# Three head pairs at the start of an attention kernel: loads on two hardware queues, rotation on VectorE, and a new order of the preparation

## The chip, the cores and the metric

The kernel runs on one core of a Trainium2 chip. The metric is the device time of one execution in microseconds (us); a time is the median of several runs. A trace of one execution tells what each engine did: PE (TensorE, matrix products and transposes; PEld is its weight loads), DVE (VectorE), ACT (ScalarE), POOL (GpSimd) and SP (SyncE, which only issues DMAs). ACT and POOL can issue DMAs too; "SPq" and "ACTq" are such issues. A difference of about 0.5% (2.6 us) is what a measurement of this kernel can tell from no change.

## The reference

Attention over 2 batches of 8 heads (sequence 576, head dimension 64) with a rotation of q and k, then a gated feed-forward block, then a second one with softmax gating and a normalisation:

```python
def rotate(x):
    x1, x2 = (x[..., :half], x[..., half:])
    return np.concatenate([x1 * cos - x2 * sin, x1 * sin + x2 * cos], axis=-1)
q_rot, k_rot = (rotate(q), rotate(k))
scores = scale * np.matmul(q_rot, k_rot.transpose(0, 1, 3, 2))
scores = scores - np.max(scores, axis=-1, keepdims=True)
attn = np.exp(scores)
attn = attn / (np.sum(attn, axis=-1, keepdims=True) + 1e-09)
return np.matmul(attn, v).astype(np.float32)
...
x = _moe_ref(x=x, **moe_kwargs)          # (x @ w_a) * (x @ w_b) @ w_out
return _moe2_ref(x=x, **moe2_kwargs)     # gated by softmax, normalised, times w_out
```

All is in float32; a product is made of three passes over values split into a high part, which TensorE takes as it is, and a low part, the rest.

## The kernel before

The 16 heads are worked on as eight pairs, numbered 0 to 7. A pair has nine blocks of 128 query rows: 0 to 3 of the first head, 5 to 8 of the second, and block 4 with the last 64 rows of both. So q and k of a pair lie in SBUF as nine blocks too, and are loaded in three parts: A (blocks 0 to 3), B (5 to 8) and R (block 4). The R part is a DMA of its own with 64 rows of each head.

Ahead of a pair's scores stands its preparation. q and k are rotated by `rope`: a product of the swapped halves with the sines into `t2`, a product with the cosines in place, and a sum. `k_hi` (ACT) and `k_lo` write the two parts of k side by side into `kd`. q is needed twice side by side in `qd`: for pairs 1 to 7 `q_twice` copies it with a DMA from SBUF to SBUF on SP's queue, for pair 0 the rotation's sum is made twice. PE then transposes `kd` and `qd` (tiles `qtkA`, `qtkB`, `qtqA`, `qtqB`, `qtR`), and ACT and DVE write the results, split, into `kS` and `qS`. In pairs 1 to 7 the rotation, `k_lo` and the low part of v run on POOL.

Then, block by block (n = 9 u + i for block i of pair u): scores `s` on PE, the row's maximum `nm` on DVE, the exponential `e` on ACT, its transposes `t` on PE, the high part of them on ACT and the low part on DVE (both into `pT`), and at four places of a pair nine products `pv` with v. At a pair's end the sums of the rows are turned into reciprocals (`sums` on DVE, `rs` on PE, `rr` on ACT), which three DMAs spread over the partitions by way of DRAM (`rd`, then `rb`, all on SP's queue); POOL multiplies the pair's output `x` with them. After the eight pairs come the feed-forward blocks, which the change leaves alone.

All of attention is put in order by hand: every step is added with a position, a number in units of one block, and all steps are sorted by it. `PLAN` holds the positions of a pair, 9 u being added; `FIRST`, `SECOND` and `THIRD` replace some for pairs 0, 1 and 2. Each engine, and each DMA queue, runs its instructions strictly in that order. The tiles `kraw`, `qd` and `kd` have two buffers each.

Before, `start` issues the loads of pair 0's k and the tables of cosines and sines (one tile `cs`), with q of pair 0 on POOL's queue, and right behind them on SP's queue the loads of pair 1 and the rest of pair 0. POOL rotates pair 1 as soon as that is there, while DVE rotates pair 0: part A and R at first, part B (`rope_k5`, `rope_q5`) between the first blocks' work.

Of the kernel before, what the change touches and what calls it, by code (L numbers as in the profile page):

```python
# [107 lines left out]
def attention_gated_ffn_solu_ffn(ctx: ExitStack, tc, q, k, v, wa, wb, wo1, wi2, wo2, gln, rope_cs, out):  # L108

    nc = tc.nc  # L110
    const = ctx.enter_context(tc.tile_pool(name="const", bufs=1))
# [65 lines left out]
    nm, e, sums, ps, tt, x0, rb = {}, {}, {}, {}, {}, {}, {}  # L177

    def load(u, nm_, parts="ABR", eng=nc.sync):

        b, h0 = u // NP, 2 * (u % NP)
        if nm_ == "k":
            src = k
            if u not in kraw:
                kraw[u] = at.tile([P, NB, D], F32, tag="kraw", name=f"kraw{u}")
            t = kraw[u]
        else:
            src = q  # L190
# [23 lines left out]
    def rope(eng, u, x, nm_, lo=0, hi=NB):  # L214
        t2 = at.tile([P, NB, D], F32, tag="t2" if u else "t2first", name=f"t2{nm_}{lo}_{u}", bufs=2 if u else 1)
        x, t2, c, s = (ap[:, lo:hi] for ap in (x, t2, c_sb, s_sb))
        swapped = x.rearrange("p b (j d) -> p b j d", j=2)[:, :, ::-1, :]
        t2, s = (ap.rearrange("p b (j d) -> p b j d", j=2) for ap in (t2, s))
        eng.tensor_tensor(t2, swapped, s, op=ALU.mult)
        t2 = t2.rearrange("p b j d -> p b (j d)")  # L220
        eng.tensor_tensor(x, x, c, op=ALU.mult)
        if nm_ == "q" and u == 0:
            eng.tensor_tensor(qd[u][:, lo:hi, 0, :], x, t2, op=ALU.add)
        eng.tensor_tensor(x, x, t2, op=ALU.add)

    def q_twice(u):
        nc.sync.dma_start(out=qd[u][:, :, 0, :], in_=qd[u][:, :, 1, :])
# [264 lines left out]
    def add(pos, fn, *args):  # L492
        ops.append((pos, len(ops), fn, args))

    def start():
# [18 lines left out]
        nc.scalar.copy(cs[:, :, 5:9], cs[:, :, 0:4])  # L514

        t = ps_t.tile([P, 4, P], F32, tag="t", name="warm")
        for i in range(28):
            nc.tensor.transpose(t[:, i % 4], ident, ident)
# [7 lines left out]
    engines = {"dve": nc.vector, "pool": nc.gpsimd}  # L526
    for part, (lo, hi) in (("0", (0, 5)), ("5", (5, 9))):
        pos = {key: FIRST[key + part] for key in ("rope_k", "k_hi", "k_lo", "rope_q")}
        add(pos["rope_k"], lambda lo, hi: rope(nc.vector, 0, kraw[0], "k", lo, hi), lo, hi)
        add(pos["k_hi"], k_hi, 0, lo, hi)  # L530
        add(pos["k_lo"], k_lo, 0, engines[HI["l" + part]], lo, hi)
        eng = engines[HI["q" + part]]
        add(pos["rope_q"], lambda lo, hi, eng: rope(eng, 0, qd[0][:, :, 1, :], "q", lo, hi), lo, hi, eng)
# [353 lines left out]
```

## Time and profile before

| | |
|---|---|
| Time, median of 3 runs | 524.66 us (524.63 to 526.62) |
| The profiled execution's own time | 524.1 us |
| Its span, first to last instruction | 522.0 us |
| Granted TensorE clock, mean | 0.986 |
| Attention | from the start to about 179 us |
| First row maximum (block 0) | starts at 16.90 us |
| First row maximum of pair 1, 2, 3 | 35.87, 56.69, 76.09 us |
| DVE busy from 40 to 60 us | 19.2 of 20 us |

A row of the timeline has start, duration, engine, line, operation, output and inputs with their shapes, the count, and in brackets how long the engine had been idle and what ended that. A row of stretches has, for each engine, its busy time and in brackets the number of its instructions, then the granted clock, the busy share of the DMA engines and what they moved.

### The profile page before, as it was taken

How to read it: one execution, taken by the hardware profiler on the slowest of the kernel's cores; microseconds unless marked ns; L12 is line 12 of the kernel's file. 1: busy time of each engine (PE TensorE's matmuls, PEld its weight loads, DVE VectorE, ACT ScalarE, POOL GpSimd, SP SyncE). 2: the span in 40 equal slices, each digit the busy share in tenths (PEclk: the TensorE clock that was granted, in tenths of full speed). 3: DMA queues.
4: the chain of work that ended last, by engine and by line, in shares of the span. 5: the costliest groups of instructions: out<-in, count | busy, mean ns of one | idle time of the engine just before them, and what ended most of it. 6: DMA issues, size and time to landing. Idle time of an engine off the chain costs nothing.

```text
span 522.0 us, 7983 instructions
## 1 busy us (share of the span) xinstructions
PE 490.2 (94%) x2992; PEld 461.7 (88%) x2992; DVE 389.7 (75%) x603; ACT 270.1 (52%) x554; POOL 178.6 (34%) x128
## 2 busy tenths in 40 slices
PE   3889989989989999999999999999999969999997
PEld 3878888989878999999999999999999858888886
DVE  5899999999999776666756656655899996755450
ACT  2698988989988535433434443321455533222221
POOL 5598987877244003211111221220054221000000
PEclk9699999999999999999999999999999989999999
DMA  6334224235003053322222221343545200100011
GB/s 147 79 94 104 67 60 109 62 74 158 24 2 105 1 161 124 119 82 82 80 83 94 76 91 62 94 148 95 180 130 162 82 0 1 40 21 21 21 40 40
DMA packets 50914, 41.97 MB, mean 80 GB/s; under 512 B 23765, under 2 KB 46868, under 8 KB 50876
## 3 DMA queue, kind: packets, MB, share of 16 engines
q1 hardware_dynamic: 50124, 40.48, 26.1%
q10 hardware_dynamic: 624, 0.82, 0.5%
q8 instruction: 23, 0.38, 0.3%
q0 software_dynamic: 128, 0.17, 0.2%
q14 instruction: 15, 0.12, 0.1%
HBM read 37.00 MB, written 2.39 MB: 75 GB/s over the span
## 4 chain that ended last, share of the span: by engine, by line
PE 70%; DVE 19%; ACT 4%; issue 3%; DMA 2%; POOL 1%; SPq 1%; ACTq 0%; POOLq 0%; DVEq 0%
PE ab L579 29%; PE x L710 10%; PE out L814 10%; PE h L743 7%; PE pv L403 5%; PE s L327 4%; DVE nm L336 3%; PE t L354 2%; DVE f L93 2%; DVE f L95 2%; ACT e L344 2%; DVE pT L372 2%; DVE f L91 1%; PE lt L785 1%; DVE V L233 1%
## 5 line engine op out<-in xcount | busy, mean ns | idle before, releaser
L579 PE MATMUL ab<-xT,wab 128*128 128x384 f32 x864 | 151.9, 336 | 0.0
L579 PEld LDWEIGHTS ab<-xT,wab 128*128 128x128 f32 x864 | 150.7, 188 | 0.1
L710 PE MATMUL x<-gT,wx 128*128 128x384 f32 x432 | 75.9, 336 | 0.0
L710 PEld LDWEIGHTS x<-gT,wx 128*128 128x128 f32 x432 | 75.6, 188 | 0.1
L104 POOL TENSOR_TENSOR wab<-f,wab 128x1024 fp32r<-128x1024 f32 x11 | 26.4, 2401 | 118.9 <-ACT wab L101 103.0
L327 PE MATMUL s<-kS,qS 128*128 128x288 f32 x320 | 60.0, 315 | 1.3 <-ACT e L344 1.2
L743 PE MATMUL h<-wh,xT 128*128 128x512 f32 x216 | 53.2, 403 | 5.0 <-DVE et L763 5.0
L344 ACT ACTIVATE e<-s,nm 128x576 f32<-128x576 f32 x72 | 53.6, 745 | 7.1 <-DVE nm L336 6.5
L336 DVE TENSOR_REDUCE nm<-s 128x1 f32<-128x576 f32 x72 | 53.7, 745 | 2.1 <-PE s L327 1.2
L743 PEld LDWEIGHTS h<-wh,xT 128*128 128x128 f32 x216 | 41.5, 193 | 15.1 <-issue 4.9
L814 PE MATMUL out<-wout,lnT 128*128 128x512 f32 (+1 forms) x240 | 52.9, 373 | 0.0
L372 DVE TENSOR_TENSOR pT<-t,pT 128x512 fp32r<-128x512 f32 x72 | 49.4, 686 | 2.4 <-ACT pT L368 1.4
L327 PEld LDWEIGHTS s<-kS,qS 128*128 128x128 f32 x320 | 47.2, 195 | 3.7 <-ACT e L344 3.0
L814 PEld LDWEIGHTS out<-wout,lnT 128*128 128x128 f32 x240 | 41.4, 188 | 7.5
L403 PE MATMUL pv<-pT,V 128*128 128x288 f32 x288 | 46.0, 304 | 0.8 <-DVE pT L390 0.7
L354 PE MATMUL t<-ident,e 128*128 128x128 f32 x288 | 44.2, 277 | 0.0
L368 ACT CAST pT<-t 128x512 fp32r<-128x512 f32 x72 | 42.2, 586 | 2.5 <-PE t L354 2.1
L403 PEld LDWEIGHTS pv<-pT,V 128*128 128x128 f32 x288 | 39.4, 188 | 2.0 <-POOL V L251 0.7
L587 ACT COPY a<-ab 128x384 f32<-128x384 f32 x36 | 17.3, 480 | 45.3 <-PE ab L579 44.6
L596 DVE TENSOR_TENSOR gT<-a,gT 128x384 fp32r<-128x384 f32 x36 | 23.1, 641 | 21.8 <-ACT gT L595 21.8
L89 DVE TENSOR_SCALAR f<-f 128x512 f32<-128x512 f32 (+2 forms) x36 | 28.7, 796 | 12.3 <-ACT f L87 12.2
L756 ACT ACTIVATE et<-h,mx 128x1024 f32<-128x1024 f32 x9 | 10.1, 1117 | 52.2 <-DVE mx L755 52.2
(132 smaller groups left out, 714.4 us busy)
## 6 DMA issues: line engine op xcount, KB each, us to landing
raw<-in_moe_w_a_dram SPq DMA_DIRECT2D x12, 512.0 KB
raw<-in_moe_w_b_dram SPq DMA_DIRECT2D x12, 512.0 KB
raw<-in_moe_w_out_dram SPq DMA_DIRECT2D x8, 768.0 KB
raw<-in_moe_w_in_dram SPq DMA_DIRECT2D x8, 512.0 KB
raw<-in_moe_w_out_dram SPq DMA_DIRECT2D x8, 512.0 KB
kraw<-in_k_dram SPq DMA_DIRECT2D x16, 128.0 KB
vraw<-in_v_dram SPq DMA_DIRECT2D x8, 256.0 KB
qd<-qd SPq DMA_DIRECT2D x7, 288.0 KB
```

What stands on the lines that cost most here:

```text
L89: eng.tensor_scalar(_raw(t), _raw(t), LOW_END, HIGH_END, op0=ALU.max, op1=ALU.min)
L327: nc.tensor.matmul(s[:, c, :KC], qS[u % 2][:, a, off:off + P], kS[u % 2][:, h, c * KC:(c + 1) * KC], start=(m == 0), stop=(m == last),)
L336: nc.vector.tensor_reduce(t, ps[n][:, :, :KC], axis=AX.XY, op=ALU.max, negate=True)
L344: nc.scalar.activation(t.rearrange("p (c n) -> p c n", c=2), ps.pop(n)[:, :, :KC], AF.Exp, bias=nm.pop(n), accum_out=sums[u][:, i:i + 1],)
L354: nc.tensor.transpose(t[:, j, :], e[n][:, j * P:(j + 1) * P], ident)
L368: nc.scalar.copy(hi, src)
L372: nc.vector.tensor_tensor(lo, src, _raw(hi), op=ALU.subtract)
L403: nc.tensor.matmul(o[:, :KC], w[:, h, 4 if m == 8 else m % 4].rearrange("p a d -> p (a d)"), t[:, m, c * KC:(c + 1) * KC], start=(m == 0), ...
L579: nc.tensor.matmul(pab[f, t][:, m, :CW], wf[:, a, m, kk, :], xT[:, kk, xa, t * CW:(t + 1) * CW], start=(kk == a == xa == 0), stop=(kk == 3 ...
L710: nc.tensor.matmul(o[:, :CW], wx[:, a], gT[f // 3, t][:, f % 3, ga], start=(f == 0 and a == ga), stop=(f == NF - 1 and a == 1),)
L743: nc.tensor.matmul(s[:, c], x2T[:, kk, xa, c0:c0 + P], wt["h", kk][:, a, c * 512:(c + 1) * 512], start=(idx == 0), stop=(idx == 11),)
L814: nc.tensor.matmul(o[:, cols], t[:, la, kk, :], w[:, a, cols], start=(kk == la == a == 0), stop=(kk == NK2 - 1 and la == 1),)
```

## The change

- The tables become two tiles, `c_sb` (half as wide, each cosine read twice) and `s_sb`, with one run of bytes for each partition. Part B of pair 0 reads the rows of part A, since its angles are the same.
- Pair 0's first loads stand on two queues: k A, cosines and q A on SP's, sines, k R and q R on ACT's. POOL issues none.
- The other loads (`later_loads`) stand behind a small `memset` of `g_sb` on DVE, into which the first of them writes: SP can issue them only after DVE has done the two products of k's rotation.
- Pair 0's rotation runs on DVE with one sum each, and part B directly behind A; only the sum of q's part B and `k_lo` of part B run on POOL. q's doubling is a copy on ACT for A and R, and a DMA for B.
- PE's warming transposes become 30, 6 and 8, in three places.
- Pairs 1 and 2 have new positions: their rotations alternate with their `k_lo`, and q's doubling, `qtqA` and `qtR` stand later.

```diff
@@ start, later_loads @@
         load(0, "k", "A")
-        nc.scalar.dma_start(out=cs[:, 1, 0:5], in_=rope_cs[:, 1])
-        load(0, "k", "R")
-        nc.sync.dma_start(out=cs[:, 0, 0:5], in_=rope_cs[:, 0])
-        load(0, "q", "A", nc.gpsimd)
+        nc.scalar.dma_start(out=s_sb[:, 0:5].rearrange("p b d -> p (b d)"), in_=rope_cs[:, 5 * D // 2:])
+        load(0, "k", "R", nc.scalar)
+        nc.sync.dma_start(out=c_sb[:, 0:5].rearrange("p b d -> p (b d)"), in_=rope_cs[:, 0:5 * D // 2])
+        load(0, "q", "A")
+        load(0, "q", "R", nc.scalar)
         make_identity(nc, ident)
-        load(0, "q", "R", nc.gpsimd)
-        load(1, "k")
-        load(0, "k", "B")
-        load(0, "q", "B")
-        load(1, "q")
-        load_v(0)
-        nc.sync.dma_start(out=g_sb, in_=gln.rearrange("(k p) -> p k", p=P))
...
+    def later_loads():
+
+        nc.vector.memset(g_sb, 0.0)
+        nc.sync.dma_start(out=g_sb, in_=gln.rearrange("(k p) -> p k", p=P))
+        load(0, "k", "B")
+        load(0, "q", "B")
+        load(1, "k")
+        load_v(0)
+        load(1, "q")
...
+    def first_k():
+        rope(nc.vector, 0, k0, "k", 0, 5, (0,))
+        later_loads()
+        rope(nc.vector, 0, k0, "k", 0, 5, (1,))
...
+        ("rope_q5", rope, nc.vector, 0, q0, "q", 5, 9, (0,)),
+        ("rope_q5_end", rope, nc.gpsimd, 0, q0, "q", 5, 9, (1,)),
...
+        ("k_lo5", k_lo, 0, nc.gpsimd, 5, 9),
@@ SECOND, THIRD @@
-    "rope_k": -11.6, "rope_q": -5.9, "q2": -5.55, "k_hi": -6.15, "k_lo": -5.65, "kA": (-4.8, -4.55),
+    "rope_k": -11.6, "rope_q": -5.2, "q2": -5.15, "k_hi": -5.5, "k_lo": -5.45, "kA": (-4.4, -4.2),
...
+    "load_k": -15.85, "load_q": -14.7, "load_v": -11.3, "rope_k": -12.8, "k_hi": -8.7, "k_lo": -8.65, "rope_q": -8.6,
+    "v_lo": -0.35, "q2": -7.4, "kA": (-7.2, -7.1), "qA": (-5.3, -5.2, -4.8), "pv11": (13.6, 13.81, 14.05, 14.2),
```

The first place is DVE from its first rotation to the first row maximum (`t2k0`, `t2q0` are the products with the sines for parts A and R, `t2k5`, `t2q5` those for B; `nm0` is the first maximum). Before:

```order
L219 TENSOR_TENSOR t2k0_0_162<-kraw0_100,cs_92 128x320
L221 TENSOR_TENSOR kraw0_100<-kraw0_100,cs_92 128x320
L224 TENSOR_TENSOR kraw0_100<-kraw0_100,t2k0_0_162 128x320
L219 TENSOR_TENSOR t2q0_0_168<-qd0_105,cs_92 128x320
L221 TENSOR_TENSOR qd0_105<-qd0_105,cs_92 128x5x64
L223 TENSOR_TENSOR qd0_105<-qd0_105,t2q0_0_168 128x5x64
L224 TENSOR_TENSOR qd0_105<-qd0_105,t2q0_0_168 128x5x64
L282 SCALAR_TENSOR_TENSOR qS0_93<-qtqA0_180,qS0_93 128x128
```

After, on the same engine at the same place:

```order
L229 TENSOR_TENSOR t2k0_0_149<-kraw0_101,s_sb_93 128x320
L230 TENSOR_TENSOR kraw0_101<-kraw0_101,c_sb_92 128x320
L529 MEMSET g_sb_72 128x8
L232 TENSOR_TENSOR kraw0_101<-kraw0_101,t2k0_0_149 128x320
L229 TENSOR_TENSOR t2q0_0_171<-qd0_102,s_sb_93 128x320
L230 TENSOR_TENSOR qd0_102<-qd0_102,c_sb_92 128x5x64
L257 TENSOR_TENSOR kd0_169<-kraw0_101,kd0_169 128x5x64
L232 TENSOR_TENSOR qd0_102<-qd0_102,t2q0_0_171 128x5x64
L229 TENSOR_TENSOR t2k5_0_191<-kraw0_101,s_sb_93 128x256
L230 TENSOR_TENSOR kraw0_101<-kraw0_101,c_sb_92 128x256
L232 TENSOR_TENSOR kraw0_101<-kraw0_101,t2k5_0_191 128x256
L229 TENSOR_TENSOR t2q5_0_195<-qd0_102,s_sb_93 128x256
```

One sum is gone, `k_lo` and part B's rotation moved ahead of the first split, and the `memset` that holds SP's queue stands third.

The second place is SP's queue around the reciprocals of pair 0 (`rd0`, `rb0`) and the doubling of q of pair 2 (`qd2<-qd2`). Before:

```order
L227 DMA qd2_319<-qd2_319 128x9x64
L196 DMA qd3_487<-in_q_dram 128x4x64 x2
L200 DMA qd3_487<-in_q_dram 128x1x64
L437 DMA rd0_520<-rr0_518 9x128
L444 DMA rb0_522<-rd0_520 64x576
L445 DMA rb0_522<-rd0_520 64x512
L446 DMA rb0_522<-rd0_520 64x64
```

After, on the same queue:

```order
L198 DMA qd3_504<-in_q_dram 128x4x64 x2
L202 DMA qd3_504<-in_q_dram 128x1x64
L452 DMA rd0_532<-rr0_530 9x128
L459 DMA rb0_534<-rd0_532 64x576
L460 DMA rb0_534<-rd0_532 64x512
L461 DMA rb0_534<-rd0_532 64x64
L235 DMA qd2_290<-qd2_290 128x9x64
```

The doubling moved from ahead of the reciprocals' four DMAs to behind them.

The third place is PE in pair 1, around the transposes of q's part A of pair 2 (`qtqA2`). Before:

```order
L327 MATMUL s11_534<-kS1_97,qS1_94 128x288 x4
L354 MATMUL t9_540<-ident_71,e9_493 128x128 x4
L265 MATMUL qtqA2_545<-ident_71,qd2_319 128x128 x4
L327 MATMUL s12_558<-kS1_97,qS1_94 128x288 x4
L354 MATMUL t10_563<-ident_71,e10_531 128x128 x4
L403 MATMUL pv100_568<-pT_95,V0_315 128x288 x9
L327 MATMUL s13_595<-kS1_97,qS1_94 128x288 x8
```

After, on the same engine:

```order
L342 MATMUL s11_553<-kS1_98,qS1_95 128x288 x4
L369 MATMUL t9_559<-ident_71,e9_510 128x128 x4
L342 MATMUL s12_571<-kS1_98,qS1_95 128x288 x4
L369 MATMUL t10_576<-ident_71,e10_549 128x128 x4
L418 MATMUL pv100_581<-pT_96,V0_329 128x288 x9
L280 MATMUL qtqA2_602<-ident_71,qd2_290 128x128 x4
L342 MATMUL s13_613<-kS1_98,qS1_95 128x288 x8
```

The transposes moved behind the scores of block 12 and the first `pv` of pair 0's second head, and stand now directly ahead of the scores of block 13.

## Rows read from the trace of the kernel before

**Rows 1.** The page: busy time of each engine, granted TensorE clock in 40 slices

```profile
PE 490.2 (94%) x2992; PEld 461.7 (88%) x2992; DVE 389.7 (75%) x603; ACT 270.1 (52%) x554; POOL 178.6 (34%) x128
...
PEclk9699999999999999999999999999999989999999
```

**Rows 2.** Stretches at the start: busy us and instructions, clock, DMA share, GB/s

```profile
9.13:12.54 3.41, 0.00 (x0) 0.00 (x0) 3.34 (x3) 0.59 (x1) 3.25 (x3) 1.00 0.52 111
...
19.37:22.78 3.41, 3.41 (x19) 3.38 (x18) 3.31 (x8) 3.03 (x7) 0.27 (x1) 0.50 0.22 77
22.78:26.19 3.41, 3.41 (x31) 3.41 (x30) 3.41 (x6) 3.28 (x9) 2.52 (x2) 1.00 0.71 155
```

**Rows 3.** Timeline up to the first row maximum

```profile
1.20 0.71 SPq L200 DMA_DIRECT2D kraw<-in_k_dram  x1
...
5.55 0.49 DVE L219 TENSOR_TENSOR t2k<-kraw,cs 128x320 f32<-128x320 f32 x1 [2.47 <-DMA kraw<-in_k_dram]
...
7.68 0.85 POOL L242 TENSOR_TENSOR kd<-kraw,kd 128x320 fp32r<-128x320 f32 x1 [4.04 <-ACT kd L231]
...
8.91 1.57 DVE L221 TENSOR_TENSOR qd<-qd,cs 128x320 f32<-128x320 f32 x1
...
13.75 1.12 PE L265 MATMUL qtqA<-ident,qd 128*128 128x128 f32 x4 [4.62 <-DVE qd L224]
...
16.90 0.76 DVE L336 TENSOR_REDUCE nm<-s 128x1 f32<-128x576 f32 x1 [0.35 <-PE s L327]
```

**Rows 4.** Timeline of the work for part B and for pairs 1 and 2

```profile
18.26 0.42 DVE L221 TENSOR_TENSOR kraw<-kraw,cs 128x256 f32<-128x256 f32 x1
...
21.75 0.69 ACT L231 CAST kd<-kraw 128x576 fp32r<-128x576 f32 x1
...
24.83 1.43 POOL L219 TENSOR_TENSOR t2k<-kraw,cs 128x576 f32<-128x576 f32 x1 [0.90 <-DMA kraw<-in_k_dram]
...
29.32 1.56 POOL L251 TENSOR_TENSOR V<-vraw,V 128x640 fp32r<-128x640 f32 x1
```

**Rows 5.** Timeline of DMA chains: loads landing, doubling of q, reciprocals of pair 0

```profile
35.56 0.64 SPq L227 DMA_DIRECT2D qd<-qd  x1
...
39.41 0.32 SPq L437 DMA_DIRECT2D rd<-rr  x1
41.48 0.51 SPq L444 DMA_DIRECT2D rb<-rd  x1
...
43.36 0.54 SPq L205 DMA_DIRECT2D vraw<-in_v_dram  x1
...
77.69 0.56 SPq L200 DMA_DIRECT2D qd<-in_q_dram  x1
...
80.72 1.43 POOL L219 TENSOR_TENSOR t2q<-qd,cs 128x576 f32<-128x576 f32 x1 [1.86 <-DMA qd<-in_q_dram]
```

**Rows 6.** Two stretches behind the doubling's issue at 35.56, columns as in Rows 2

```profile
36.80:37.20 0.40, 0.40 (x6) 0.40 (x5) 0.40 (x2) 0.40 (x2) 0.40 (x2) 1.00 0.81 173
37.20:37.60 0.40, 0.40 (x7) 0.40 (x6) 0.40 (x1) 0.40 (x2) 0.40 (x1) 1.00 1.05 215
```

**Rows 7.** Timeline from the first `pv` to block 14, and one earlier cast

```profile
25.56 1.04 DVE L233 CAST V<-vraw 128x640 fp32r<-128x640 f32 x1
...
31.70 1.43 PE L403 MATMUL pv<-pT,V 128*128 128x288 f32 x9 [0.53 <-DVE pT L390]
...
36.91 1.52 DVE L422 TENSOR_SCALAR sums<-sums 128x9 f32<-128x9 f32 x1
...
44.00 1.22 PE L327 MATMUL s<-kS,qS 128*128 128x288 f32 x8
...
45.26 0.76 DVE L336 TENSOR_REDUCE nm<-s 128x1 f32<-128x576 f32 x1
...
47.43 0.76 DVE L336 TENSOR_REDUCE nm<-s 128x1 f32<-128x576 f32 x1 [0.19 <-PE s L327]
48.10 0.48 DVE L233 CAST V<-vraw 128x640 fp32r<-128x640 f32 x1
```

More of the change, by code (lines that the diff above doesn't have):

```diff
@@ L44 @@
 FIRST = {
[4 rows of a table removed]
[6 rows of a table added]
 }
 SECOND = {
-    "rope_k": -11.6, "rope_q": -5.9, "q2": -5.55, "k_hi": -6.15, "k_lo": -5.65, "kA": (-4.8, -4.55),
-    "qA": (-3.0, -2.95, -2.35), "load_q": -10.1, "R": (-3.65, -3.55, -3.2), "x_hi": 17.05, "load_k": -19.1,
-    "v_hi": -2.6, "pv11": (13.15, 13.61, 14.05, 14.2), "exp": 0.85, "pv01": (8.5, 8.71, 9.35, 9.55),
-    "pv00": (7.7, 7.86, 8.0, 8.75),
+    "rope_k": -11.6, "rope_q": -5.2, "q2": -5.15, "k_hi": -5.5, "k_lo": -5.45, "kA": (-4.4, -4.2),
+    "qA": (-1.35, -1.3, -0.7), "load_q": -10.1, "R": (-1.65, -1.6, -1.2), "kB": (-2.6, -2.5), "x_hi": 17.05,
+    "load_k": -19.1, "v_hi": -2.9, "v_lo": 1.0, "pv11": (13.15, 13.61, 14.05, 14.2), "exp": 0.85,
+    "pv01": (8.5, 8.71, 9.35, 9.55), "pv00": (7.7, 7.86, 8.0, 8.75),
 }
 THIRD = {
-    "load_k": -15.85, "load_q": -13.2, "load_v": -11.3, "k_hi": -10.05, "k_lo": -10.0, "v_lo": -0.35, "q2": -9.8,
-    "pv11": (13.6, 13.81, 14.05, 14.2),
+    "load_k": -15.85, "load_q": -14.7, "load_v": -11.3, "rope_k": -12.8, "k_hi": -8.7, "k_lo": -8.65, "rope_q": -8.6,
+    "v_lo": -0.35, "q2": -7.4, "kA": (-7.2, -7.1), "qA": (-5.3, -5.2, -4.8), "pv11": (13.6, 13.81, 14.05, 14.2),
 }
-HI = {"k": "act", "v": "dve", "x": "pool", "l0": "pool", "l5": "dve", "q0": "dve", "q5": "dve", "r": "act"}
+HI = {"k": "act", "v": "dve", "x": "pool", "r": "act"}
 AB = (72.45, 72.81, 73.22, 73.33, 76.45, 77.46, 77.57, 77.93)
@@ L176, in attention_gated_ffn_solu_ffn @@
     kraw, vraw, kd, qd, V, qt, po = {}, {}, {}, {}, {}, {}, {}
-    nm, e, sums, ps, tt, x0, rb = {}, {}, {}, {}, {}, {}, {}
+    nm, e, sums, ps, tt, x0, rb, t2s = {}, {}, {}, {}, {}, {}, {}, {}
     def load(u, nm_, parts="ABR", eng=nc.sync):
@@ L212, in load_v, with halves, rope, q_twice @@
             )
[L214 to L227, printed above, removed]
+    def halves(ap):
+        return ap.rearrange("p b (j d) -> p b j d", j=2)
+    def rope(eng, u, x, nm_, lo=0, hi=NB, steps=(0, 1)):
+        if 0 in steps:
+            t2s[nm_, u, lo] = at.tile(
+                [P, NB if u else 5, D], F32, tag="t2" if u else "t2first", name=f"t2{nm_}{lo}_{u}", bufs=2
+            )
+        t2, x = t2s[nm_, u, lo][:, 0:hi - lo], x[:, lo:hi]
+        if 0 in steps:
+            rows = slice(0, hi - lo) if u == 0 else slice(lo, hi)
+            c = c_sb[:, rows].unsqueeze(2).to_broadcast([P, hi - lo, 2, D // 2])
+            eng.tensor_tensor(halves(t2), halves(x)[:, :, ::-1, :], halves(s_sb[:, rows]), op=ALU.mult)
+            eng.tensor_tensor(halves(x), halves(x), c, op=ALU.mult)
+        if 1 in steps:
+            eng.tensor_tensor(x, x, t2, op=ALU.add)
+    def q_twice(u, lo=0, hi=NB):
+        nc.sync.dma_start(out=qd[u][:, lo:hi, 0, :], in_=qd[u][:, lo:hi, 1, :])
+    def q_first_twice():
+        nc.scalar.copy(qd[0][:, 0:5, 0, :], qd[0][:, 0:5, 1, :])
+    def angles_twice():
+        for t in (c_sb, s_sb):
+            nc.scalar.copy(t[:, 5:9], t[:, 0:4])
     def copy(eng, dst, src):
@@ L513, in start, with warm @@
             nc.scalar.copy(t[:, :, 576:640], zero)
[L514 to L518, printed above, removed]
+        warm_t.append(ps_t.tile([P, 4, P], F32, tag="t", name="warm"))
+        warm(30)
+    def later_loads():
[6 more added lines that the diff above has]
+        load(1, "q")
+    def warm(n):
+        for i in range(n):
+            nc.tensor.transpose(warm_t[0][:, i % 4], ident, ident)
+    warm_t = []
     ident_r = ac.tile([P, P], F32R, name="ident_r")
@@ L525, in attention_gated_ffn_solu_ffn @@
             add(pos, q_part, 0, fn, *cols)
[L526 to L533, printed above, removed]
+    kraw[0] = k0 = at.tile([P, NB, D], F32, tag="kraw", name="kraw0")
+    qd[0] = at.tile([P, NB, 2, D], F32, tag="qd", name="qd0")
+    q0 = qd[0][:, :, 1, :]
+    def first_k():
+        rope(nc.vector, 0, k0, "k", 0, 5, (0,))
+        later_loads()
+        rope(nc.vector, 0, k0, "k", 0, 5, (1,))
+    for key, fn, *args in (
+        ("rope_k0", first_k),
+        ("k_hi0", k_hi, 0, 0, 5),
+        ("rope_q0", rope, nc.vector, 0, q0, "q", 0, 5, (0,)),
+        ("k_lo0", k_lo, 0, nc.vector, 0, 5),
+        ("rope_q0_end", rope, nc.vector, 0, q0, "q", 0, 5, (1,)),
+        ("q_twice0", q_first_twice),
+        ("cs5", angles_twice),
+        ("rope_k5", rope, nc.vector, 0, k0, "k", 5, 9),
+        ("rope_q5", rope, nc.vector, 0, q0, "q", 5, 9, (0,)),
+        ("rope_q5_end", rope, nc.gpsimd, 0, q0, "q", 5, 9, (1,)),
+        ("k_hi5", k_hi, 0, 5, 9),
+        ("q_twice5", q_twice, 0, 5, 9),
+        ("k_lo5", k_lo, 0, nc.gpsimd, 5, 9),
+        ("warm1", warm, 6),
+        ("warm2", warm, 8),
+    ):
+        add(FIRST[key], fn, *args)
     for u in range(NU):
@@ L859, in _tables @@
     rows = np.concatenate([np.arange(REM).reshape(P, 4), np.tile(np.arange(REM, S), 2)[:, None]], 1)
-    return np.ascontiguousarray(
-        np.stack([np.concatenate([cos, cos], -1)[rows], np.concatenate([-sin, sin], -1)[rows]], 1)
-    )
+    tables = cos[rows].reshape(P, -1), np.concatenate([-sin, sin], -1)[rows].reshape(P, -1)
+    return np.ascontiguousarray(np.concatenate(tables, 1))
 _INS = ["q", "k", "v", "moe_w_a", "moe_w_b", "moe_w_out", "moe2_w_in", "moe2_w_out", "moe2_g_ln"]
```

4 lines of the change are left out of this document (2 added, 2 removed), and 10 rows, old and new, of the table FIRST.

## The prediction

> **What bounds the kernel now.** I read the page first, then stretches, the timeline at the start, and last the timeline of DMA issues. In the page PE is busy for 490.2 of 522.0 us, DVE for 389.7 [rows 1]: behind attention PE never rests, so whatever moves the end of attention moves the end of the kernel by as much. In attention itself DVE has no room: between 40 and 60 us it works for 19.2 of 20. The start is another matter. The first row maximum begins at 16.90, and ahead of it PE waits 4.62 us for the rotation of q on DVE [rows 3]. That rotation is slow: a product of 320 columns takes 1.57 us where the same size took 0.49 at 5.55 [rows 3]; in those microseconds POOL works 3.25 of 3.41 us [rows 2], on pair 1. PE has no matmul at all in that stretch, its clock falls to 1.2 GHz and is back at 2.4 GHz only after 22.78: with PE busy throughout, 19 matmuls fit into 3.41 us before that point and 31 behind it [rows 2]. So the start loses time in a way that the change goes for. The question is whether the next stages can take the gain.
>
> **The first rotation.** k's part R is issued at 1.20, and the first product starts at 5.55 when it has landed [rows 3]. An R load of the steady part goes from issue (77.69) to its reader (80.72) in 3.03 us [rows 5]. So the new start lies between 1.20 + 3.03 = 4.2 and 5.55. With q off POOL's queue, but q A and q R added to the same transfers, I take 5.2, nearer to what this very load needed. The Trainium skill (DMA: Bandwidth & Descriptors, Issuing engines are not separate DMA queues) speaks against a gain here: issuing from several engines saves only the time of issuing, as all share the same 16 DMA engines. By this rule the start would stay at 5.55 and the sum would be 0.35 us longer.
>
> From 5.2 two products (0.49 each and some 0.04 between, [rows 3]) and the `memset` bring DVE to 6.35; only then does SP issue on. The table for `g_sb` takes some 0.6 to issue (its neighbours take 0.5 [rows 5]), so k's part B is issued at 7.0. No row has such a load by itself; a transfer of 4.5 KB needs 2.07 (39.41 to 41.48) and an R load 3.03 [rows 5]. I take 2.75, nearer to the load: it lands at 9.75. Meanwhile DVE does the sum, q's A and R without POOL beside it, at 0.49 instead of 1.57, and `k_lo`, and is free at 8.9: the held loads leave it idle for 0.85 us. The removed sum for q's double, 1.57 beside POOL and 0.49 without, only lengthens that idle time. Then five passes over 256 columns at 0.42 [rows 4] and 0.04 between: 12.1. Behind them stand the three splits of q, 640 columns, so some 1.05 at the same rate: the first row maximum starts near 13.2 instead of 16.90. That gain, 3.7 us, is real but is not yet the kernel's.
>
> **Pair 1.** POOL's preparation used to start ahead of all this, beside DVE. Now two more steps stand in front: q's last sum, which waits for 12.1, and `k_lo` of part B. A POOL pass costs 0.85 for 320 columns [rows 3], so 0.68 for 256: POOL is at 13.5. k of pair 1 takes 4.5 (24.83 to 29.32 [rows 4]), the cast on ACT 0.7 [rows 4], `k_lo` 1.4 and q 4.5: 24.65. Only then can SP issue q's doubling. Before, such an issue at 35.56 set the DMA engines to work from about 36.8, at 215 GB/s [rows 5, 6]: 1.25 us, 288 KB in 1.35, and the end's notice, for which 0.7 is an estimate (what is left of the 2.07 of the small transfer when the 1.25 is taken off, about 0.8). So 3.3 us, and 28.0. Bounds are 2.6 (no notice) and 3.9 (the load of k behind it shares the engines). In the new order `qtR1` stands ahead of the first `pv`, behind the transposes of block 5. Pair 0 took 18.97 us from its first maximum to that of pair 1 (16.90 to 35.87); without eight passes of 0.42 for part B that is 1.73 a block, so PE is there by about 25 (13.2 + 5 x 1.73, and some 3 for the exponential and the transposes behind a maximum) and waits 3 us. `pv` starts at 28.35 instead of 31.70 [rows 7]: of 3.7 us, 3.35 are left.
>
> From there to the issue of the reciprocals it took 39.41 - 31.70 = 7.7 us [rows 5, 7]. In the new order the transposes of q A (0.4 on PE) and the cast of pair 2's k (0.7 on ACT [rows 4]) stand in that stretch, side by side; I take 0.5 for both. `sums`, nine columns, took 1.52 there [rows 7], which depends on where POOL is; I take 0.4 off, an estimate. That makes 7.8, and the issue at 36.15, 3.25 us earlier.
>
> **Pair 2 gives it back.** In SP's order the doubling of q of pair 2 was ahead of the reciprocals and is now behind them. POOL is no limit: after V's low part (1.5) and k of pair 2 it stands at 30.7, waits for ACT's cast, now behind pair 0's last exponentials, until about 33.5 (an estimate, 2.6 ahead of the reciprocals), and has q at 33.5 + 1.4 + 4.5 = 39.4. But SP waits for `rd` (2.07) and issues three `rb` (41.48 to 43.36: 1.88) [rows 5], then 3.3 for the copy: 36.15 + 7.25 = 43.4. PE needs it for `qtqA2`, directly ahead of the scores of block 13. Without the wait PE would get there at 44.00 - 3.25 - 0.45 = 40.3, by the start of block 13's scores before [rows 7] less the gain and the transposes. So it waits 3.1 us, does the transposes (0.45) and starts block 13 at 43.85: 0.15 us earlier than before. Behind that DVE is full again, with the split of q A (0.6) now behind block 13's maximum (45.26 before [rows 7]) where it stood ahead of it; PE's wait of 0.19 at 47.43 goes. Block 14's maximum thus starts where it did, 47.4. And V's cast behind it took 0.48 because POOL paused just there; beside POOL such a cast takes 1.04 [rows 7], and POOL is now in q of pair 3. That is 0.55 more. From there both kernels have the same work on a full DVE.
>
> **The sum:** 3.7 (first maximum) - 0.35 (to the first `pv`) - 0.1 (to the reciprocals) - 3.1 (at `qtqA2`) - 0.15 (the split behind it) - 0.55 (V's cast) = -0.55, so half a microsecond slower: 524.1 + 0.5 = 524.6 for the profiled execution. The median of the runs shown lies 0.56 above that execution, so 525.2. PE's warming transposes (44 against 28) and the smaller tables cost nothing: PE waits there anyway.
>
> **Rivals.** *The gain is kept.* If the doubling of pair 2 lands before PE needs it, 3.25 us stay: 521.4. It decides by 7.25 us of DMA chain against the 4.2 that PE needs from the reciprocals to `qtqA2`. For it speaks that DVE may still have maxima to do while PE waits; against it that DVE's 45.26 followed PE's scores almost at once [rows 7]. *The clock falls.* PE's two waits of 3 us are nearly as long as its rest ahead of 13.75, 4.62 us [rows 3], behind which the clock was at 1.2 GHz until 22.78. If a copy lands later and one of the waits reaches that length, PE does 19/31 of its work for some 10 us [rows 2]: 3.9 us, less the 6% of the time that PE rests [rows 1], 0.6, and 0.4 more for the later landing. 525.2 + 3.7 = 528.9. It decides somewhere between waits of 3 and 4.6 us. *The loads gain nothing.* k's part R lands no sooner on ACT's queue, since q A and q R take the place that pair 1's loads had, and the first product starts at 5.55 as before: all later points move by 0.35, to 525.5. The page's rule above would have it so.
>
> **How the numbers follow.** The forecast of 525.2 has 0.60, the kept gain 0.25, the fallen clock 0.10, loads that gain nothing 0.05. The forecast's own range follows from its unknown terms: the first landing (1.0 less, 0.35 more), part B's (0.7 less, 1.1 more), two copies (0.7 less each, 0.6 more), V's cast (0.55 less): not all at one end, so 523.0 to 527.2. With the kept gain within it the range is 521.0 to 527.4; a fall of the clock and a tenth for better than the kept gain stay outside. 0.5% is 2.6 us, about what a measurement of this kernel can tell from no change: below 522.0 lies the kept gain, 0.25; above 527.3 the fallen clock and the forecast's tail, 0.13; the rest, 0.62, is the same.
>
> **What would show it.** In the timeline of the new kernel: first row maximum near 13.2 (right for the start); POOL's first pass over pair 1 near 13.5 and q of pair 1 done near 24.7; PE idle some 3 us ahead of `qtR1`, and again ahead of `qtqA2`, with the second wait put down to a DMA; the maximum of block 9 near 33 and that of block 18 back at about 57 (56.69 before). If block 18 stands near 53.5, the kept gain is right and the wait at `qtqA2` was not the limit. A granted clock of 0.5 between 25 and 50 us shows the clock's rival. The forecast is wrong altogether if POOL's chain starts much earlier than 13.5, since all else hangs on it.

## The result: slower by 0.85%

The changed kernel takes 530.35 us (median of 10 executions, 528.22 to 531.58), the kernel before 524.85 (524.46 to 526.86): a ratio of 1.0085, 95% interval 1.0068 to 1.0103. The prediction was 525.2, range 521.0 to 527.4. The profiled execution took 528.44 with a span of 526.5, 4.5 us more than before; it is among the faster third of its kernel, so the trace shows a little less of the loss than the median.

All of the 4.5 us is in attention. The last row maximum starts at 174.34 instead of 169.80, and behind it both spans have 352.2 us left. The starts of the row maxima on DVE (before against after, us) show where:

| Block | 0 | 5 | 7 | 8 | 9 | 12 | 13 | 14 | 18 | 27 | 71 |
|---|---|---|---|---|---|---|---|---|---|---|---|
| before | 16.90 | 27.13 | 32.78 | 34.05 | 35.87 | 43.24 | 45.26 | 47.43 | 56.69 | 76.09 | 169.80 |
| after | 11.69 | 21.24 | 25.47 | 30.98 | 34.47 | 41.91 | 48.50 | 51.99 | 61.23 | 80.64 | 174.34 |
| difference | -5.2 | -5.9 | -7.3 | -3.1 | -1.4 | -1.3 | +3.2 | +4.6 | +4.5 | +4.6 | +4.5 |

The start gains more than forecast, up to 7.3 us. Then 5.9 us are lost twice: from block 7 to 9, and from block 12 to 14.

### The profile page after: what moved, and what is told of

It is laid out like the page before. It is cut to its first block, busy times and chain, and to the rows that moved or that the text cites. A ratio compares the mean times of both kernels' runs of the same rounds, so it can differ in the third digit from the quotient of the medians.

```text
span 526.5 us, 8017 instructions
## 1 busy us (share of the span) xinstructions
PE 493.9 (94%) x3008; PEld 464.4 (88%) x3008; DVE 384.2 (73%) x601; ACT 270.0 (51%) x556; POOL 176.4 (34%) x127
## 4 chain that ended last, share of the span: by engine, by line
PE 69%; DVE 16%; ACT 4%; issue 4%; POOL 3%; DMA 2%; SPq 0%; ACTq 0%; POOLq 0%; DVEq 0%
PE ab L620 29%; PE x L751 10%; PE out L855 9%; PE h L784 7%; PE pv L418 5%; PE s L342 4%; PE t L369 2%; DVE f L95 2%; DVE f L97 2%; DVE nm L351 2%; ACT e L359 2%; DMA kraw<-in_k_dram 2%; DVE pT L387 1%; DVE f L93 1%; PE lt L826 1%
## 5 line engine op out<-in xcount | busy, mean ns | idle before, releaser
L342 PEld LDWEIGHTS s<-kS,qS 128*128 128x128 f32 x320 | 46.9, 194 | 3.6 <-ACT e L359 3.5
L97 DVE SCALAR_TENSOR_TENSOR f<-raw,f 128x512 int32<-128x512 int32 (+2 forms) x36 | 36.4, 1012 | 0.9
```

The lines of the kernel that those rows point to most:

```text
L97: eng.scalar_tensor_tensor(t, lo, 29, t, op0=ALU.logical_shift_right, op1=ALU.bitwise_or)
L342: nc.tensor.matmul(s[:, c, :KC], qS[u % 2][:, a, off:off + P], kS[u % 2][:, h, c * KC:(c + 1) * KC], start=(m == 0), stop=(m == last),)
```

## The profile after

The start, on DVE (timeline rows as in [rows 3]):

```profile
4.87 0.49 DVE L229 TENSOR_TENSOR t2k<-kraw,s_sb 128x320 f32<-128x320 f32 x1 [3.30 <-DMA kraw<-in_k_dram]
...
8.72 0.42 DVE L229 TENSOR_TENSOR t2k<-kraw,s_sb 128x256 f32<-128x256 f32 x1 [0.58 <-DMA kraw<-in_k_dram]
...
11.69 0.76 DVE L351 TENSOR_REDUCE nm<-s 128x1 f32<-128x576 f32 x1
```

The first product starts at 4.87 instead of 5.55, part B keeps DVE waiting for 0.58, and PE's wait of 4.62 us is gone. k's part R, for which that product waited, is issued no sooner than before (1.19 against 1.20), so what was saved is not issue time. The tables' new layout, q off POOL's queue and the second queue changed together, and no run separates them.

The first loss, on PE and on ACT:

```profile
24.07 0.30 PE L274 MATMUL qtR<-ident_r,kd 128*128 128x128 f32 x1
26.75 0.30 PE L280 MATMUL qtR<-ident,qd 128*128 128x128 f32 x1 [2.38 <-DMA qd<-qd]
26.87 0.90 PE L418 MATMUL pv<-pT,V 128*128 128x288 f32 x5
27.91 1.11 PE L280 MATMUL qtqA<-ident,qd 128*128 128x128 f32 x4
28.68 1.31 PE L418 MATMUL pv<-pT,V 128*128 128x288 f32 x4
29.78 1.16 PE L342 MATMUL s<-kS,qS 128*128 128x288 f32 x4
```

```profile
27.08 0.27 ACT L314 CAST kS<-qtR 128x128 fp32r<-128x128 f32 x1 [1.71 <-PE qtR L280]
...
29.06 0.60 ACT L293 ACTIVATE qS<-qtqA 128x512 fp32r<-128x512 f32 x1 [1.05 <-PE qtqA L280]
30.02 0.40 ACT L425 COPY tmp0pv<-pv 64x288 f32<-64x288 f32 x1 [0.36 <-PE pv L418]
30.44 0.74 ACT L359 ACTIVATE e<-s,nm 128x576 f32<-128x576 f32 x1
...
34.42 0.68 ACT L246 CAST kd<-kraw 128x576 fp32r<-128x576 f32 x1
```

PE waits 2.38 us for q's double. The scores of block 8 (29.78) stand behind it. On ACT steps that follow from the wait (27.08, 29.06 and 30.02 among them) stand ahead of block 7's exponential: its maximum started at 25.47, the exponential only at 30.44. The cast of pair 2's k, behind that, comes at 34.42, and POOL had been waiting for it:

```profile
28.18 1.41 POOL L232 TENSOR_TENSOR kraw<-kraw,t2k 128x576 f32<-128x576 f32 x1
35.18 1.42 POOL L257 TENSOR_TENSOR kd<-kraw,kd 128x576 fp32r<-128x576 f32 x1 [5.59 <-ACT kd L246]
...
39.55 1.42 POOL L232 TENSOR_TENSOR qd<-qd,t2q 128x576 f32<-128x576 f32 x1
```

This hole of 5.59 us makes q of pair 2 late (off POOL at 39.55 + 1.42 = 40.97), and pair 3's k too. SP, from the reciprocals on:

```profile
37.61 0.31 SPq L452 DMA_DIRECT2D rd<-rr  x1
39.98 0.52 SPq L459 DMA_DIRECT2D rb<-rd  x1
...
41.98 0.66 SPq L235 DMA_DIRECT2D qd<-qd  x1
```

The second loss, on PE, and the rows of ACT and DVE beside it:

```profile
40.74 1.45 PE L418 MATMUL pv<-pT,V 128*128 128x288 f32 x9
45.52 1.08 PE L280 MATMUL qtqA<-ident,qd 128*128 128x128 f32 x4 [3.33 <-DMA qd<-qd]
46.26 2.21 PE L342 MATMUL s<-kS,qS 128*128 128x288 f32 x8
...
50.01 1.42 PE L418 MATMUL pv<-pT,V 128*128 128x288 f32 x9 [1.10 <-DVE qS L297]
```

```profile
46.64 0.60 ACT L293 ACTIVATE qS<-qtqA 128x512 fp32r<-128x512 f32 x1 [4.41 <-PE qtqA L280]
47.13 0.73 ACT L359 ACTIVATE e<-s,nm 128x576 f32<-128x576 f32 x1
...
49.18 0.68 DVE L297 SCALAR_TENSOR_TENSOR qS<-qtqA,qS 128x512 fp32r<-128x512 f32 x1
```

Behind the wait of 3.33 us stand the scores of block 13, the exponential of block 12 (maximum at 41.91, exponential at 47.13), and a `pv` that waits 1.10 more: `qtqA` holds one of the two buffers that these tiles share until DVE has split it, at 49.18. None of them needs q of pair 2, whose first scores are block 18.

Last the clock, in stretches (columns as in [rows 2]):

```profile
24.00:27.00 3.00, 0.62 (x6) 0.46 (x5) 2.15 (x4) 0.83 (x2) 2.92 (x3) 1.00 0.56 120
28.00:31.00 3.00, 3.00 (x14) 2.98 (x15) 0.71 (x2) 1.56 (x4) 1.51 (x2) 0.50 0.40 103
42.00:44.00 2.00, 0.19 (x2) 0.00 (x0) 1.25 (x2) 0.23 (x1) 1.92 (x3) 1.00 0.60 156
45.00:48.00 3.00, 2.48 (x11) 2.51 (x12) 0.00 (x0) 1.34 (x4) 2.92 (x3) 0.50 0.31 94
```

In each wait PE is nearly idle. The granted clock is 0.50, which is 1.2 GHz, from 27.8 to 31.2 and from 44.9 to 48.3 (read in stretches of half a microsecond), so from about a microsecond behind the end of the first wait and from just ahead of the end of the second. The scores of block 13 take 2.21 us, 1.22 before.

## The experiments

All are measured beside the kernel before; "end" is the start of the last row maximum against 169.80. One profile shows a mechanism; the ratio is over 4 to 10 executions beside 12 to 30 of before. The profile of before took 524.1 us and its medians beside the experiments are 525.46 to 526.07, so "end" reads up to 2 us worse than the ratio. The diffs of positions show only the entries that differ.

### Each half alone

`e3_first_only` is the changed kernel with `SECOND` and `THIRD` of before, `e4_orders_only` the kernel before with both tables of the changed one.

> The changed kernel with SECOND and THIRD of before: only the new start is left. Theory 1 (the start gains, the new positions of pairs 1 and 2 give it away): pair 1's q is rotated ahead of its k_lo, done near 21.2, its double lands near 24.5; PE meets qtkA ahead of block 5 and waits there some 4 us for k_lo (22.6), then some 1 to 2 us for the double; block 7's maximum is some 3 to 4 us earlier than before (32.78), pair 2's double lands near 36.5, ahead of its need, and the rest keeps this gain: 520.5 to 522. Theory 2 (the new start brings nothing that pair 1 can use, whatever the positions): block 9's maximum within 0.5 of 35.87 and 524 to 526.

> The kernel before with SECOND and THIRD of the changed one: the old start, the new positions. Theory 1 (the new positions lose time at both places whatever the start): k_hi of pair 1 on ACT near 22, so k_lo and q on POOL from 23 to 29, the double lands near 32; PE waits 2 to 3 us at qtR1, block 9's maximum 3 to 4 us behind 35.87; then a second wait at qtqA2; block 14's maximum 7 to 10 us behind 47.43 and 531 to 534. Theory 2 (the positions are harmless without the new start): block 14's maximum within 2 us of 47.43, and 524 to 527.

`e3`: 0.9954 (0.9936 to 0.9972), end -0.40. The new start alone is a small gain. Block 3's maximum is still 6.8 us earlier than before; 2.1 of that go by block 4, where PE waits 1.67 for an exponential, and 4.1 by block 6, around PE's wait for `k_lo` of pair 1, which in the old order stands ahead of block 5:

```profile
23.07 0.70 PE L274 MATMUL qtkA<-ident_r,kd 128*128 128x128 f32 x4 [2.75 <-POOL kd L257]
```

The clock is at 1.2 GHz there, from 23.2 to 26.6. Block 6's maximum is only 0.58 earlier than before: theory 1 was too hopeful on how much is kept (its time was 520.5 to 522, the median is 523.50), and block 9's (35.22) is near where theory 2 had it. `e4`: 1.0177 (1.0143 to 1.0210), end +10.05 over four executions, as theory 1 said and a little worse, with waits of 2.33 at `qtR` and 3.4 at `qtqA`. So the new positions lose the time, and without the new start they lose more. The halves do not simply add: -0.46% and +1.77% alone, +0.85% together.

### The clock

In `qt_pe`, ahead of q's transposes for `qtR` and for `qtqA`:

```diff
+            if u == 1:
+                for i in range(22):
+                    nc.tensor.transpose(o[:, 2 * P:3 * P], ident, ident)
...
+            if (u, key) == (2, "qA"):
+                for i in range(32):
+                    nc.tensor.transpose(o[:, 0:P], ident, ident)
```

> The changed kernel with PE's two waits filled: 22 transposes of the identity ahead of qtR1's transposes of q and 32 ahead of qtqA2's, written into columns that are overwritten or unused. Theory 1 (the loss is what stands behind the two doubles; the clock is a small part): the granted clock stays at 1.0 behind both waits, and the time falls by 1 us or less against the changed kernel, 527.5 to 528.5. Theory 2 (most of the loss is the clock of 1.2 GHz behind each wait): the clock stays up and the time falls by 3 to 4.5 us, to 524 to 525.5. If the clock falls all the same, the run says nothing on its price.

1.0020 (1.0003 to 1.0037), end +1.94. The same stretches:

```profile
28.00:31.00 3.00, 1.93 (x16) 1.69 (x15) 2.07 (x4) 2.49 (x6) 1.42 (x1) 1.00 0.34 100
...
45.00:48.00 3.00, 1.90 (x16) 1.69 (x15) 2.04 (x4) 2.95 (x7) 2.92 (x3) 1.00 0.00 1
```

With PE busy where it waited, the clock stays up. That gives back 2.6 us in the profile (1.45 by block 9, the rest by block 14) and 0.65% in the ratios, some 3.4 us, give or take 1.3 by the two intervals: between the two theories, nearer to the second. That is most of the net loss, of which some 1 us (1.0020) stays, but not most of what is lost at the two places: with the clock up, 4.6 us still go from block 7 to 9 and 4.7 from block 12 to 14, where it was 5.9 each.

### The first place

```diff
-    "qA": (-1.35, -1.3, -0.7), "R": (-1.65, -1.6, -1.2),
+    "qA": (-0.84, -0.7, -0.3), "R": (-0.85, -0.8, -0.4),
```

> The changed kernel with the steps R and qA of pair 1 later: PE's transposes at 8.15 instead of 7.35 and 7.65, behind the scores of block 8 and the first pv; ACT's splits at 8.2 and 8.3 instead of 7.4 and 7.7, behind block 7's exponential; DVE's at 8.6 and 8.7. Theory 1 (the first loss comes from what stood behind the late double in PE's and ACT's queues: block 8's scores, pv and block 7's exponential): PE waits less than 0.5 us at qtR1, block 9's maximum falls from 34.47 to about 31, the second wait stays, and the time is 3 to 4 us below the changed kernel, near 525. Theory 2 (what waits is only moved: pair 1's first scores need the double anyway, and its landing sets them): block 9's maximum at 33.5 or later, time within 1 us of the changed kernel.

1.0008 (0.9987 to 1.0028), end +2.18. Block 9's maximum is at 31.11, no wait at `qtR`, no fall of the clock there: theory 1. Of the 5.9 us lost from block 7 to 9, 2.6 stay; PE now waits for the low part of v, which POOL makes behind q of pair 1:

```profile
25.27 1.46 PE L418 MATMUL pv<-pT,V 128*128 128x288 f32 x9 [0.96 <-POOL V L266]
```

The second wait stays (3.5 us), and the clock is at 1.2 GHz around it, from 43.6 to 50.4.

### The second place

`x1_q2_ahead` moves only pair 2's `q2`, `x2_khi_early` only its `k_hi` and `k_lo`, `x3_pair2_early` both:

```diff
-    "k_hi": -8.7, "k_lo": -8.65, "q2": -7.4,
+    "k_hi": -10.05, "k_lo": -10.0, "q2": -7.6,
```

> The changed kernel with one step moved: q2 of pair 2 at 10.4, ahead of the reciprocals on SP; k_hi stays late. Theory 1 (two chains of nearly equal length make the double late: POOL has q only at 41.0 because ACT's cast k_hi comes at 34.4, and SP is free only at 41.98): the issue moves by 1 us to 41.0, the landing to 44.5, PE still waits over 2 us at qtqA2, block 14's maximum is near 51 instead of 51.99, and the time within 1.5 us of the changed kernel. Theory 2 (the place behind the reciprocals is what makes it late, as the prediction had it): the wait is gone, 5 us less.

> The changed kernel with only k_hi and k_lo of pair 2 at -10.05 and -10.0; q2 stays behind the reciprocals on SP. Theory 1 (two chains): POOL has q near 36.5, but SP issues the double only behind the three rb, near 42, it lands near 45.3, PE waits over 2.5 us at qtqA2 and the time is within 1 us of the changed kernel. Theory 2 (ACT's late cast alone makes it late): the wait is gone and the time is 5 us less.

> The changed kernel with k_hi and k_lo of pair 2 back at -10.05 and -10.0 (as before) and its q2 at -7.6, so ahead of the reciprocals on SP; all else as changed. Theory 1 (the second loss is the late double of pair 2, and it takes both ACT's cast and SP's order to make it late): POOL has q near 36.2, the double lands near 39.7, PE doesn't wait at qtqA2, block 14's maximum is near 46.5 and not 51.99, and the time is some 5.5 us below the changed kernel, near 523. Theory 2 (the second loss has another cause, the order of DVE and ACT there, or the clock that fell behind the first wait): block 14's maximum stays behind 50 and the time is above 526.5.

`x1`: the double is issued at 41.48, and PE still waits 1.99:

```profile
44.69 0.63 PE L280 MATMUL qtqA<-ident,qd 128*128 128x128 f32 x4 [1.99 <-DMA qd<-qd]
```

The end is at +4.37, with the clock down for 6.8 us behind the wait. By the ratio, 1.0019 (0.9998 to 1.0040), it gives back more than its profile shows: that execution took 528.71, the median is 527.26. So theory 1's time, within 1.5 us of the changed kernel, holds by the profile and not by the ratio.

`x2`: POOL has q at 36.02, but PE waits 4.47, longer than in the changed kernel, since SP issues at 42.56; 1.0079 (1.0052 to 1.0105), end +5.14:

```profile
46.10 1.09 PE L280 MATMUL qtqA<-ident,qd 128*128 128x128 f32 x4 [4.47 <-DMA qd<-qd]
```

`x3`: no wait, block 13 at 43.87, 0.9976 (0.9961 to 0.9990), end -0.05. Block 14 came at 47.36, 0.9 later than expected: `pv` still waits 1.1 for the buffer that `qtqA` holds.

Two chains of nearly equal length make the double late, ACT's cast through POOL and the reciprocals on SP. With the place on SP mended its issue is 0.5 us earlier (1.0 when both are counted from block 12's maximum, which in this profile is 0.5 later), with ACT's cast mended it is 0.6 later, and with both mended it is at 37.40 and the wait is gone. What `x1` alone is worth stays open between its two measures.

The step can also be moved instead of the data (`f1_pair2_qa_late`, the first diff), and ACT's cast of pair 3's k with it (`f2_pair2_and_khi3`, the second):

```diff
-    "qA": (-5.3, -5.2, -4.8),
+    "qA": (-3.9, -3.88, -3.65),
```

```diff
-    "qA": (-5.3, -5.2, -4.8),
+    "qA": (-2.7, -2.5, -2.3),
+FOURTH = {"k_hi": -10.6}
```

> The changed kernel with one step moved: qtqA of pair 2 and its two splits at 14.1, 14.12 and 14.35 instead of 12.7, 12.8 and 13.2, so behind the second pv of that place; block 18 is the first that needs them. q2 stays where it is, behind the reciprocals. Theory 1 (the second loss is only the place of this step, ahead of scores, an exponential and a pv that don't need it): no PE wait over 0.5 us at qtqA2, block 13's maximum near 44, block 14's near 46 instead of 51.99, attention's last maximum near 168.5, and 5.5 to 6 us below the changed kernel, 522 to 523.5. Theory 2 (the doubling itself is too late for pair 2, wherever it is read): block 18's maximum stays behind 58 and the time within 2 us of the changed kernel.

> The changed kernel with qtqA of pair 2 at 15.3 (splits at 15.5 and 15.7), behind t4R, and ACT's cast k_hi of pair 3 at 16.4 instead of 13.35. Theory 1 (with qtqA out of the way, ACT's cast for pair 3 waits for POOL's rotation of its k until 47.2, and that took the rest): nothing waits over 1 us between block 12 and block 18, block 18's maximum is 1 to 1.7 us earlier than before (56.69), so 55 to 55.7, and 522.5 to 524. Theory 2 (another limit stands behind): block 18's maximum at 58 or later.

`f1`: block 13 at 43.57, as theory 1 had it, but 1.0020 (1.0004 to 1.0036) and end +4.34 (its profiled execution took 529.21, the median is 527.48). A new wait took its place, of ACT for POOL, which is late by the hole at 30 us; PE waits behind it, and the clock is at 1.2 GHz from 49.8 to 56.6:

```profile
47.19 0.67 ACT L246 CAST kd<-kraw 128x576 fp32r<-128x576 f32 x1 [2.90 <-POOL kraw L232]
```

```profile
50.98 1.03 PE L393 MATMUL t4A<-ident,e 128*64 128x128 f32 x4 [3.38 <-DVE x L432]
```

`f2`: that wait is gone too, 0.9996 (0.9983 to 1.0010), end +1.28; block 14 is 1.6 earlier than before, and 2.9 are lost from there to block 18; PE's waits of 0.96, 0.37 and 0.67 are 2.0 of them. Block 18 came at 57.93: at least 2.2 us later than theory 1 had it, close to the 58 of theory 2.

### The hold of the later loads

`h1_loads_not_held` issues them right behind the first loads, without the `memset`.

> The changed kernel without the hold: the later loads are issued right behind the first ones, with no memset ahead of them. Theory 1 (the hold shields the first loads and little else, what it gives at the start it takes at part B): the first product starts at 5.2 to 5.8 instead of 4.87, part B waits for nothing at 8.72, the first maximum comes within 0.4 of 11.69, and the time is within 1 us of the changed kernel. Theory 2 (the hold is what makes the start fast): the first maximum is 1.5 us later or more, 13.2 or more. Theory 3 (the hold delays the loads of pair 1 and so POOL's chain): POOL's first pass over pair 1 starts before 12.33 and the double of pair 1 lands over 0.5 us before 26.7.

1.0074 (1.0049 to 1.0099). First product at 4.94, DVE waits 0.36 for q instead of 0.58 for part B, first maximum at 12.07, pair 1's first pass on POOL at 12.19: theory 1. The hold is worth next to nothing: the ratio is that of the changed kernel within both intervals. In this profile the end is at +7.16; PE's second wait is 4.01 there, 0.7 longer, and the clock is at 1.2 GHz for 10 us around and behind it.

### Keeping the gain

`b1_both_mended` has q of pair 1 ahead of its `k_lo` on POOL, and both places mended; `b2_three_places` moves `qtqA` of pair 2 once more, ACT's cast for pair 3 and POOL's product with the reciprocals too; `b3_readers_late` moves the readers of pair 3 (`qtkA`, `qtqA`) and puts pair 2's doubling behind the reciprocals again; `b3_x_last` leaves POOL's product where it was. The last one against the changed kernel, only the entries that differ:

```diff
 FIRST  + "pv00": (7.55, 7.86, 8.0, 8.22)
 SECOND - "rope_q": -5.2, "q2": -5.15, "k_lo": -5.45, "kA": (-4.4, -4.2), "qA": (-1.35, -1.3, -0.7)
 SECOND + "rope_q": -5.48, "q2": -5.47, "k_lo": -5.3, "kA": (-2.75, -2.6), "qA": (-0.95, -0.9, -0.75)
 THIRD  - "k_hi": -8.7, "k_lo": -8.65, "rope_q": -8.6, "qA": (-5.3, -5.2, -4.8)
 THIRD  + "k_hi": -9.1, "k_lo": -9.05, "rope_q": -9.0, "qA": (-2.7, -2.5, -2.3)
 FOURTH + "k_hi": -10.6, "q2": -10.05, "kA": (-6.0, -5.9), "qA": (-5.3, -5.2, -4.75)
```

> The changed kernel with both places mended: POOL rotates q of pair 1 ahead of its k_lo, qtkA of pair 1 stands at 6.25 behind that, its split of qA on ACT at 7.95; pair 2's k_hi at 9.07, its q2 at 10.4 ahead of the reciprocals, its qtqA at 14.1. Theory 1 (the start is worth up to 7 us at block 7's maximum, and pair 1's double is what it can be used up to): the double lands near 24.4 when PE gets there, block 9's maximum is near 29.5 (35.87 before), no wait at qtqA2, block 18's near 51 (56.69 before), so 4.5 to 6.5 us below before: 518.5 to 520.5. Theory 2 (POOL's and ACT's work for pairs 1 and 2 caps the gain near 1 us as in the changed kernel): block 9's near 34, block 18's near 55, 522.5 to 524.

> b1 with three places more: qtqA of pair 2 at 15.3, k_hi of pair 3 at 16.4, POOL's product with the reciprocals of pair 0 ahead of q of pair 3; and pair 1's qtqA behind block 8's scores, its splits behind block 7's exponential and ahead of block 8's low part, k_hi of pair 2 at 8.9. Theory 1 (POOL's late steps, read too early by ACT and PE, cap the gain): block 9's maximum at 30 to 31.5, block 18's at 51.5 to 53, the rest as before, so 4 to 5 us below before, 519 to 521. Theory 2 (POOL itself has no room, whatever the order): block 18's maximum within 1.5 us of 56.69 and 523.5 to 525.5.

> b2 with the double of pair 2 behind the reciprocals again, qtkA and qtqA of pair 3 at 21.0 and 21.7 instead of 19.25 and 20.15, and its doubling behind the loads of pair 4's k. Theory 1 (the gain is lost where ACT and PE read POOL's results too early, pair after pair): no wait over 1 us for POOL or for a double up to block 27, block 18's maximum at 52.5 to 53.5 (56.69 before), block 27's 3 to 4 us earlier than 76.09, attention ends near 166, and 520 to 522. Theory 2 (POOL has no room: its work from 11 us on decides): another wait for POOL before block 36 and its maximum within 1.5 us of 95.49, 523.5 to 526.

> b3 with POOL's product with the reciprocals of pair 0 behind q of pair 3 again, as in the changed kernel. Theory 1: pair 1's first sum on DVE waits for x of pair 0 to be free, 2 to 4 us, near 52; the rest as b3, 522 to 524. Theory 2 (the order on POOL doesn't matter): same time as b3 within 1 us.

| Kernel | Block 9 | Block 15 | Block 18 | Block 27 | End | Ratio (95%) |
|---|---|---|---|---|---|---|
| `b1` | -3.4 | -0.2 | -0.1 | 0.0 | 0.0 | 0.9984 (0.9968 to 1.0000) |
| `b2` | -3.5 | -4.2 | -3.5 | +1.6 | +1.6 | 0.9969 (0.9949 to 0.9990) |
| `b3` | -3.7 | -4.4 | -3.0 | -1.3 | -1.3 | 0.9945 (0.9924 to 0.9967) |
| `b3_x_last` | -4.9 | -5.1 | -4.3 | -2.6 | -2.6 | 0.9943 (0.9922 to 0.9964) |

`b1` and `b2` lost the gain where ACT and PE read POOL's late results:

```profile
43.34 0.67 ACT L246 CAST kd<-kraw 128x576 fp32r<-128x576 f32 x1 [1.52 <-POOL kraw L232]
```

```profile
57.37 0.54 PE L275 MATMUL qtkA<-ident_r,kd 128*128 128x128 f32 x4 [2.84 <-POOL kd L258]
```

With the readers moved back, `b3` and `b3_x_last` kept more of it, though POOL has the same work, so POOL does have room; several positions changed at once, and which of them matters most was not separated. `b1`, `b2` and `b3` kept less than their theory 1 had, which was 518.5 to 520.5, 519 to 521 and 520 to 522; the medians are 525.12, 525.04 and 522.59. Part of what `b1` and `b2` lost there is the clock, at 1.2 GHz from 46.9 to 50.3 in `b1` and from 58.6 to 62.0 in `b2`.

`b3_x_last` was expected slower than `b3` and is not (522.48 against 522.59): POOL's order at that place doesn't matter. The 1.2 us between them at block 9 in the table come ahead of that place, where in `b3` the clock is at 1.2 GHz from 24.05 to 27.5. Of the 4.3 us that `b3_x_last` has at block 18, 1.7 go by block 23, 1.10 of them visible as the old wait of a `pv` for a split, now of pair 3. Its granted clock is 1.00 from 12 to 65 us. At 522.48 against 525.46 us it beats the kernel before, and by the two ratios (0.9943 and 1.0085) the changed one too:

```profile
30.97 0.76 DVE L352 TENSOR_REDUCE nm<-s 128x1 f32<-128x576 f32 x1 [0.67 <-PE s L343]
...
52.39 0.70 DVE L352 TENSOR_REDUCE nm<-s 128x1 f32<-128x576 f32 x1
...
73.51 0.70 DVE L352 TENSOR_REDUCE nm<-s 128x1 f32<-128x576 f32 x1
```

## Why the prediction was wrong

**The first rotation: right in kind, too small.** 13.2 was forecast, 11.69 came. Part B landed for DVE at 8.72 instead of 9.75, and the first load sooner as well. By the rule of the Trainium skill (DMA: Bandwidth & Descriptors, Issuing engines are not separate DMA queues) the start would have stayed at 5.55; the trace has 4.87, and `h1`, without the hold, 4.94. That does not refute the rule, since the tables and q's queue changed as well; it shows only that the hold is not the cause.

**Pair 1 up to the wait: right.** q off POOL at 23.5 (forecast 24.65), the double 3.23 us behind its issue (3.3), PE's wait 2.38 (3).

**From the first `pv` to the reciprocals: the term that failed most.** The forecast took 7.7 us from the trace of before, 7.8 with its additions; it was 37.61 - 26.87 = 10.74. A wait on PE was taken as a shift of everything behind it. But ACT's splits wait with PE, with block 7's exponential behind them in its queue, block 8's scores stand behind PE's wait, and the clock falls. With the clock kept up (`c1`) the stretch is 9.42, from 26.73 to 36.15: of the 2.9 us too much some 1.3 are the clock. `r2` moved only these steps and started block 9's maximum 3.4 us earlier.

**The doubling of pair 2: right place, wrong chain.** It was issued at 41.98 (forecast 40.1), landed after 3.5 us (3.3), and PE waited 3.33 (3.1). The working blamed SP's order and called POOL no limit, with ACT's cast at about 33.5 and q done at 39.4; the cast came at 34.42, POOL was done only at 40.97, and `x1` and `x2` show that either chain alone keeps the double late.

**Behind the second wait: failed.** From the start of block 13's scores to block 14's maximum 3.55 us were forecast; it took 51.99 - 46.26 = 5.73. In `c1`, with the clock up, it is 4.83 (44.54 to 49.37), so 0.9 of the 2.2 us too much are the clock; the rest is put down to ACT's exponential behind the split and to the `pv` that waited 1.10 for the buffer, which `c1` still has. How it divides between these two was not tested.

**V's cast** was forecast at 0.55 more and costs nothing: it took 0.48 (at 52.67), with POOL idle beside it from 51.15 to 53.71.

The sum, step by step: 1.5 more gained at the start, 2.9 lost from `pv` to the reciprocals, 1.0 more to block 13's scores, 2.2 behind them, 0.55 not lost at the cast: the forecast -0.55 becomes -4.6.

**Rivals.** The fallen clock had 0.10 and a price of 3.7 us, of which `c1` gives 2.6 to 3.4. Its condition was wrong: it was to decide between waits of 3 and 4.6 us, and waits of 2.38 and 3.33 were enough. The kept gain did not happen, but `b3_x_last` (3.0 us in the medians) shows that it was there to be had, with other positions.

## What to carry to other kernels

When a result comes later to an engine that runs in order, ask of every engine in its chain what stands behind the waiting step in its queue, and whether that needs the result; a wait of 2 to 3 us cost 5.9 here. A wait of PE has a second price, the clock behind it, and filling the wait with idle transposes shows that price in one run. Look at the reader's place as well as at the data: q of pair 2 was read five blocks before anything needed it. Moving that reader alone (`f1`, 1.0020) gave back less here than bringing the data earlier (`x3`, 0.9976), since POOL's late work then held up the next step; with ACT's cast of pair 3 moved too (`f2`) it was 0.9996.
